# Moving operands of the two dense layers begin at twelve other columns, in tiles 128 columns wider

## The chip, the cores and the metric

The kernel runs on one core of a Trainium2 chip. The metric is the device time of one execution in microseconds; lower is better. The kernel before was run three times.

## The reference

Three stages follow each other. The first is a recurrent attention over 768 steps for 4 batches and 8 heads of 48; its result, 3072 tokens by 384, goes through two dense layers with 2048 hidden columns each.

```python
for t in range(S):
    cur = np.einsum('bhd,bhe->bhde', u[None] * kt, vt)
    y[:, :, t] = np.einsum('bhd,bhde->bhe', rt, state + cur)
    state = wt[:, :, :, None] * state + np.einsum('bhd,bhe->bhde', kt, vt)
...
h = x @ w_in;  g = np.maximum(h, 0.0) + alpha * np.minimum(h, 0.0);  x = g @ w_out
h = x @ w_in;  g = h * np.clip(h + 3.0, 0.0, 6.0) / 6.0;             out = g @ w_out
```

## The kernel before

**Tiling.** Tokens run in six blocks of 512 (`TB`), j = 0 to 5, through each of the two dense layers, m = 0 and 1. The 2048 hidden columns run in 16 slices of 128. Every float32 operand of a dense product is split into a high part, rounded to the format float32r, and the low rest, so that one product of 128 rows by 128 columns of weights with 512 tokens is three matmuls in `mm3` (lines 765 to 767): high by high, high by low, low by high. A slice of a block ("slot") needs three row groups of `x` for its hidden tile `h` (nine matmuls) and three column groups for its output `acc` (nine more). That makes 18 matmuls a slot, 288 a block, 1728 a layer.

**Operands.** The weights stay in 32 tiles of [128, 2, 384] 4-byte words, high and low part one behind the other, which the second layer's weights later replace. The moving operands are the activation tiles `xt` and `x2` of [128, 3, 2, 512] (two buffers, tag "xt"), and the gate tile `g` of [128, 2, 512] (three buffers). In each matmul the stationary operand is a 128-column piece of a weight tile, loaded by an LDWEIGHTS of its own while the matmul ahead of it streams its 512 columns.

**Where the tiles lie.** All pools lie one behind the other along each partition, and the widths between the first weight tile and the tiles that stream are multiples of 128 words (768 a weight tile, 384 a work tile, 512 a staging tile, 3072 an activation tile, 4 x 544 for the tiles ahead of `g`). So each moving operand of a dense layer and each 128-column piece of weights begin at the same column, counted modulo 128. Below, "distance" is the first column of the streaming operand less the first column of the weights that are loaded meanwhile, modulo 128: it is 0 for all 3456 dense matmuls. Other pairs have other distances. When a burst of attention follows a dense matmul, the next weights are a state tile `sbd` of 112 columns (line 588, `y<-kr,sbd`), and the four of these tiles stand at distances 120, 8, 24 and 40 from the streaming `xt`.

**Order.** The order of all instructions is made beforehand by a planner (`Plan`) from costs and due times; each engine then runs its own list. During layer 0 the attention of the next block (units of 256 tokens by two heads) is woven between the slots: `A<-kr` (line 477), `y<-kr,sbd` (588), `y<-X,v` (595, 599). A result `y` is split into the two parts of `xt` by ACT (635) and DVE (641), and a quarter of it goes there by DMA (651). In each slot ACT and DVE turn `h` into `g` (lines 801 or 803, 808 or 812, 818, 821) while PE works on other slots. From line 699 on, checks of the weights' range run during layer 0, from loads of their own.

Of the kernel before, what the change touches and what calls it, by code (L numbers as in the profile page):

```python
# [8 lines left out]
F32R = mybir.dt.float32r  # L9
# [11 lines left out]
P = 128  # L21
# [9 lines left out]
NK = DM // P  # L31
# [5 lines left out]
TB = 512  # L37
NB = NT // TB
AHEAD = 8
WARM = 400  # L40
FUSE = 16
U0, U1, W0 = -3.9, 2.0, -0.82


# [72 lines left out]
class Plan:  # L117
# [42 lines left out]
    def run(self):  # L160
        ops = self.ops
        for o in ops:
            o["left"] = len(o["full"]) + len(o["order"])
            for d in o["full"] | o["order"]:
                ops[d]["out"].append(o["id"])
        ready = {e: [] for e in ("PE", "DVE", "ACT", "POOL", "SP")}
        free = {e: self.BEGIN[e] for e in ready}

        def release(o):
            at = {e: 0.0 for e in o["where"]}  # L170
            for d in o["full"]:
                p = ops[d]
                for e in o["where"]:
                    wait = self.SAME[e] if e == p["eng"] else self.LATENCY
                    at[e] = max(at[e], p["end"] + wait)
            for d in o["order"]:
                for e in at:
                    at[e] = max(at[e], ops[d]["start"])
            o["t"] = at
            for e in o["where"]:  # L180
                ready[e].append(o)

        for o in ops:
            if not o["left"]:
                release(o)
        seq = []
        pair = 0.0

        def earliest(e, o):
            t = max(free[e], o["t"][e])  # L190
            return max(t, pair) if e == "POOL" or (e == "DVE" and o["pair"]) else t

        while True:
            best = None
            for e, lst in ready.items():
                if lst:
                    t = min(earliest(e, o) for o in lst)
                    if best is None or t < best[0]:
                        best = (t, e)
            if best is None:  # L200
                break
            t, e = best
            o = min(
                (o for o in ready[e] if earliest(e, o) <= t),
                key=lambda o: (o["due"] + (self.SPARE if o["flex"] and e == "DVE" else 0), o["id"]),
            )
            for x in o["where"]:
                ready[x].remove(o)
            d = o["where"][e] * (2 if e == "PE" and t < self.COLD else 1)
            o["eng"], o["start"], o["end"] = e, t, t + d  # L210
            free[e] = t + d
            if self.LOCK and (e == "POOL" or (e == "DVE" and o["pair"])):
                pair = t + d
            if e == "SP":
                o["end"] = t + d + 2.0
            if not (o.get("filler") and self.started):
                seq.append(o)
            else:
                o["end"] = t
                free[e] = t  # L220
            if o.get("starts"):
                self.started = True
            for x in o["out"]:
                ops[x]["left"] -= 1
                if not ops[x]["left"]:
                    release(ops[x])
        return seq


def fast_path(es, tc, unit, tok, vch, ub, w1, w2, alpha, out, flag, alp, x2d):  # L230
# [4 lines left out]
    xp = es.enter_context(tc.tile_pool(name="xp", bufs=2))  # L235
# [68 lines left out]
    XT, xt_buf, xt_ops = {}, {}, {}  # L304
# [49 lines left out]
    def add_unit(n):  # L354
        t, pr = divmod(n, NPAIR)
# [248 lines left out]
        def add_output(due=d + 2, more=0.0, then=None, after=(), use=()):  # L604

            def both(e):
                pc(e)
                if then:  # L610
                    then(e)

            o_pc = plan.op(
                {"PE": (0.8 if first else 1.02) + more}, due, both, need + list(after), new=[yb2],
                use=[krb, xb, vb] + sb + list(use),
            )

            j, off = t // 2, t % 2 * TH
            if j not in xt_buf:
                xt_buf[j] = plan.buf("xt", 2)  # L620
            ops = xt_ops.setdefault(t, [])
            cs = slice(off, off + TH)
            x3b = plan.buf("x3", 1) if pr == 3 else None

            def parts():
                if j not in XT:
                    XT[j] = xp.tile([P, NK, 2, TB], F32R, tag="xt", name=f"xt{j}")
                if pr < 3:
                    return XT[j][0:PR, pr, 0, cs], XT[j][0:PR, pr, 1, cs]
                if "x3" not in u:  # L630
                    u["x3"] = ap_.tile([PR, 2, TH], F32R, tag="x3", bufs=1, name=f"x3_{t}")
                return u["x3"][:, 0], u["x3"][:, 1]

            def hi_(e):
                nc.scalar.activation(
                    parts()[0], u["y"], AF.Copy, accum_out=sum_y[0:PR, n : n + 1]
                )

            def lo_(e):
                hi, lo = parts()  # L640
                nc.vector.tensor_tensor(out=lo, in0=u["y"], in1=hi.bitcast(F32), op=ALU.subtract)

            fresh = [xt_buf[j]] + ([x3b] if x3b else [])
            o_hi = plan.op({"ACT": 0.36}, d + 2.5, hi_, [o_pc], new=fresh, use=[yb2])
            o_lo = plan.op({"DVE": 0.35}, d + 2.5, lo_, [o_hi], new=fresh, use=[yb2])
            ops += [o_hi, o_lo]

            if pr == 3:

                def spread(e, h, i):  # L650
                    nc.sync.dma_start(
                        XT[j][48 + 64 * h : 64 + 64 * h, i, :, cs].bitcast(F32),
                        u["x3"][64 * h + 16 * i : 64 * h + 16 * i + 16].bitcast(F32),
                    )

                before = list(ops)
                for h in range(2):
                    for i in range(NK):
                        ops.append(
                            plan.op(  # L660
                                {"SP": 0.48}, d + 2.6, lambda e, h=h, i=i: spread(e, h, i),
                                before, use=[xt_buf[j], x3b],
                            )
                        )
            return o_pc

        if FUSE <= n + 1 < NU:
            waiting.append(add_output)
# [92 lines left out]
    acc_t, acc_buf, X2, x2_ops, x2_buf, x2d_ops = {}, {}, {}, {}, {}, {}  # L761
# [7 lines left out]
    def add_slot(m, j, f):  # L769
# [6 lines left out]
        k = {}  # L776
# [18 lines left out]
        def fresh(tag, bufs, shape, dtype=F32):  # L795
            return mp.tile(shape, dtype, tag=tag, bufs=bufs, name=f"{tag}{s}")
# [17 lines left out]
                )  # L814

        def ghi(e):
            k["g"] = fresh("g", 3, [P, 2, TB], F32R)
            nc.scalar.activation(k["g"][:, 0], k["p"], AF.Copy)  # L818

        def glo(e):  # L820
# [4 lines left out]
        o_q = plan.op({"ACT": 0.58}, s + 1.1, pq, [o_h, o_alpha], new=[qb], use=[hb])  # L825
        o_g = plan.op({"DVE": 0.62}, s + 0.8, gate, [o_q], new=[pb], use=[qb, hb])
        o_1 = plan.op({"ACT": 0.52}, s + 1.0, ghi, [o_g], new=[gb], use=[pb])
        o_2 = plan.op({"POOL": 1.23, "DVE": 0.61}, s + 1.2, glo, [o_1], use=[pb, gb], pair=True)

# [42 lines left out]
    def add_x2(j):  # L872
        due = NB * NF + NF * j - 6
        x2_buf[j] = plan.buf("xt", 2)
        x2_ops[j] = []
        for i in range(NK):
            sb = plan.buf("st", 4)
            k = {}

            def load(e, i=i, k=k):  # L880
                k["raw"] = xp.tile([P, TB], F32, tag="st", bufs=4, name=f"x2r{j}_{i}")
                nc.sync.dma_start(k["raw"], x2d[j, i])

            def hi(e, i=i, k=k):
                if j not in X2:
                    X2[j] = xp.tile([P, NK, 2, TB], F32R, tag="xt", name=f"x2_{j}")
                nc.scalar.activation(X2[j][:, i, 0], k["raw"], AF.Copy)

            def lo(e, i=i, k=k):
                xt = X2[j]  # L890
                eng[e].tensor_tensor(
                    out=xt[:, i, 1], in0=k["raw"], in1=xt[:, i, 0].bitcast(F32), op=ALU.subtract
                )

            o = plan.op({"SP": 0.75}, due + i, load, [x2d_ops[0, j, i]], new=[sb])
            o = plan.op({"ACT": 0.52}, due + 1 + i, hi, [o], new=[x2_buf[j]], use=[sb])
            o2 = plan.op(
                {"POOL": 1.25, "DVE": 0.61}, due + 2.2 + i, lo, [o], use=[x2_buf[j], sb]
            )
            x2_ops[j] += [o, o2]  # L900
# [291 lines left out]
```

## Time and profile before

| | us |
|---|---|
| median of 3 runs | 952.91 (952.12 to 954.6) |
| the profiled execution | 951.98 |
| its span in the profile | 950.1 |
| PE busy | 921.2 (97%) |
| DVE busy, ACT busy | 558.2, 531.8 |

What lies outside the span is 1.9 us. The 40 slices of the page show PE near full in all but the first; the granted clock of TensorE is full from the start of the dense layers to the last slice. ACT and DVE are about two thirds busy in the first half and one third in the second, in which only the second dense layer runs (about 543 to 945 us).

### The profile page before, as it was taken

The page shows a single profiled execution, that of the slowest core. Times are in us where ns is not written, and L with a number is a line of the kernel's source. Part 1 is how long each engine was busy: PE and PEld are TensorE (multiplying, and loading weights), DVE is VectorE, ACT ScalarE, POOL GpSimd, SP SyncE. Part 2 cuts the span into 40 slices and gives each one's busy share as a digit, 9 for nine tenths or more (in the row PEclk, how much of TensorE's full clock was granted, in tenths as well). Part 3 has the DMA queues.
Part 4 walks back from the last instruction along what each step waited for, and adds up shares of the span by engine and source line. Part 5 has one row for each costly group of instructions (what it writes and reads, how often), then busy time and mean ns, then how long its engine had stood idle before and what let it go on. Part 6 is the DMA issues. An engine that isn't in the chain of part 4 may idle for free.

```text
span 950.1 us, 13762 instructions
## 1 busy us (share of the span) xinstructions
PE 921.2 (97%) x4914; PEld 744.5 (78%) x4914; DVE 558.2 (59%) x1085; ACT 531.8 (56%) x1267; POOL 133.0 (14%) x133
## 2 busy tenths in 40 slices
PE   8799989999999999989999999999999999999996
PEld 5676767878887888777888888888888888888885
DVE  8999997565655656665359887343343433433332
ACT  6888776565656657877368886343333433433331
POOL 4323234121121201000012130000010000000000
PEclk9999999999999999999999999999999999999998
DMA  8788214122212215772046630010100100100001
GB/s 269 244 271 260 83 54 144 55 80 80 95 63 70 96 55 180 224 225 60 9 163 194 192 117 1 1 67 1 38 29 1 67 1 1 67 1 1 33 1 38
DMA packets 36750, 86.20 MB, mean 91 GB/s; under 512 B 5056, under 2 KB 7488, under 8 KB 36672
## 3 DMA queue, kind: packets, MB, share of 16 engines
q1 hardware_dynamic: 36672, 85.22, 28.6%
q8 instruction: 41, 0.67, 0.3%
q14 instruction: 37, 0.30, 0.1%
HBM read 73.41 MB, written 9.44 MB: 87 GB/s over the span
## 4 chain that ended last, share of the span: by engine, by line
PE 53%; DMA 4%; DVE 2%; ACT 1%; issue 1%; DVEq 0%; ACTq 0%
PE acc L765 9%; PE acc L766 9%; PE acc L767 9%; PE h L765 9%; PE h L766 9%; PE h L767 9%; DMA raw<-in_w 4%; DVE wv L112 1%; ACT junk L710 0%; DVE pg L808 0%; PE y L595 0%; DVE g L821 0%; PE A L477 0%; PE y L588 0%; DVE X L499 0%
## 5 line engine op out<-in xcount | busy, mean ns | idle before, releaser
L765 PE MATMUL acc<-g,w 128*128 128x512 f32 x576 | 228.9, 397 | 0.0
L767 PE MATMUL acc<-g,w 128*128 128x512 f32 x576 | 224.6, 390 | 0.0
L766 PE MATMUL acc<-g,w 128*128 128x512 f32 x576 | 224.5, 390 | 0.0
L821 DVE TENSOR_TENSOR g<-pg,g 128x512 fp32r<-128x512 f32 x175 | 122.7, 701 | 139.5 <-ACT g L818 139.4
L818 ACT ACTIVATE g<-pg 128x512 fp32r<-128x512 f32 x192 | 120.8, 629 | 146.4 <-PE acc L767 142.2
L803 ACT ACTIVATE q<-h,three 128x512 f32<-128x512 f32 x96 | 66.1, 688 | 123.8 <-PE h L767 123.8
L812 DVE SCALAR_TENSOR_TENSOR pg<-q,h 128x512 f32<-128x512 f32 x96 | 65.9, 687 | 112.3 <-ACT q L803 112.1
L765 PEld LDWEIGHTS acc<-g,w 128*128 128x128 f32 x576 | 108.1, 188 | 23.5 <-issue 0.4
L767 PEld LDWEIGHTS acc<-g,w 128*128 128x128 f32 x576 | 108.1, 188 | 22.8
L766 PEld LDWEIGHTS acc<-g,w 128*128 128x128 f32 x576 | 108.2, 188 | 21.5 <-DVE g L821 0.3
L765 PE MATMUL h<-xt,w 128*128 128x512 f32 x288 | 116.2, 404 | 1.5 <-ACT w L738 1.4
L767 PE MATMUL h<-xt,w 128*128 128x512 f32 x288 | 113.2, 393 | 0.2 <-DVE w L742 0.2
L766 PE MATMUL h<-xt,w 128*128 128x512 f32 x288 | 112.2, 390 | 0.0
L808 DVE SCALAR_TENSOR_TENSOR pg<-h,q 128x512 f32<-128x512 f32 x96 | 66.0, 688 | 78.4 <-ACT q L801 78.4
L765 PE MATMUL h<-x,w 128*128 128x512 f32 x288 | 112.0, 389 | 0.0
L766 PE MATMUL h<-x,w 128*128 128x512 f32 x288 | 112.0, 389 | 0.0
L767 PE MATMUL h<-x,w 128*128 128x512 f32 x288 | 112.0, 389 | 0.0
L801 ACT ACTIVATE q<-h,nal 128x512 f32<-128x512 f32 x96 | 65.4, 682 | 58.8 <-PE h L767 58.5
L423 POOL TENSOR_TENSOR kr<-un,tg 112x512 f32<-112x512 f32 (+1 forms) x43 | 43.4, 1012 | 233.0 <-PE y L588 201.5
L765 PEld LDWEIGHTS h<-xt,w 128*128 128x128 f32 x288 | 54.9, 191 | 13.0 <-ACT w L738 2.1
L767 PEld LDWEIGHTS h<-xt,w 128*128 128x128 f32 x288 | 54.0, 188 | 13.6 <-DVE w L742 1.7
L765 PEld LDWEIGHTS h<-x,w 128*128 128x128 f32 x288 | 54.1, 188 | 11.3
(93 smaller groups left out, 1268.1 us busy)
## 6 DMA issues: line engine op xcount, KB each, us to landing
wraw<-in_w SPq DMA_DIRECT2D x64, 384.0 KB, 3.9
un<-in_unit SPq DMA_DIRECT2D x48, 337.3 KB, 3.4
raw<-in_w SPq DMA_DIRECT2D x32, 384.0 KB, 3.7
rk<-in_tok SPq DMA_DIRECT2D x24, 384.0 KB, 3.9
v<-in_vch SPq DMA_DIRECT2D x12, 384.0 KB, 3.7
x2d<-st SPq DMA_DIRECT2D x18, 256.0 KB, 2.3
x2r<-x2d SPq DMA_DIRECT2D x18, 256.0 KB, 3.2
out<-st SPq DMA_DIRECT2D x18, 256.0 KB, 2.1
```

The lines of the kernel that those rows point to most:

```text
L112: nc.vector.tensor_scalar(v, weight_bits(raw)[0], 27, 15, op0=ALU.logical_shift_right, op1=ALU.bitwise_and)
L423: eng[e].tensor_tensor(out=u["kr"][:, i].rearrange("p a (c s) -> p a c s", c=2), in0=u["in"][:, 0 : 2 * TH].rearrange("p (a c s) -> p a c ...
L765: nc.tensor.matmul(ps, whi, xhi, start=start, stop=False, skip_group_check=True)
L766: nc.tensor.matmul(ps, whi, xlo, start=False, stop=False, skip_group_check=True)
L767: nc.tensor.matmul(ps, wlo, xhi, start=False, stop=stop, skip_group_check=True)
L801: nc.scalar.activation(q, k["h"], AF.Relu, scale=nal[:, f : f + 1])
L803: nc.scalar.activation(q, k["h"], AF.Relu, bias=three)
L808: nc.vector.scalar_tensor_tensor(out=p, in0=k["h"], scalar=0.0, in1=k["q"], op0=ALU.max, op1=ALU.subtract)
L812: nc.vector.scalar_tensor_tensor(out=p, in0=k["q"], scalar=6.0, in1=k["h"], op0=ALU.min, op1=ALU.mult)
L818: nc.scalar.activation(k["g"][:, 0], k["p"], AF.Copy)
L821: eng[e].tensor_tensor(out=k["g"][:, 1], in0=k["p"], in1=k["g"][:, 0].bitcast(F32), op=ALU.subtract)
```

## The change

Both kinds of moving tile become 128 words wider, and each block takes its operand from another start within the tile. `SHIFT` gives the start for layer m and block j. The weights stay where they are, and the wider tiles move the tiles behind them by multiples of 128 words, so the value in `SHIFT` is the new distance: 4, 8, 112, 0, 120, 124 for the blocks of layer 0, and 16, 32, 48, 64, 80, 96 for those of layer 1. The block j = 3 of layer 0 keeps distance 0. Both `xt` or `x2` and the `g` tiles of a block have the block's distance.

```diff
+SHIFT = ((4, 8, 112, 0, 120, 124), (16, 32, 48, 64, 80, 96))
...
+def shifted(tile_, m, j, n):
+
+    return tile_[:, SHIFT[m][j] : SHIFT[m][j] + n]
...
-                    XT[j] = xp.tile([P, NK, 2, TB], F32R, tag="xt", name=f"xt{j}")
+                    xt = xp.tile([P, NK * 2 * TB + P], F32R, tag="xt", name=f"xt{j}")
+                    XT[j] = shifted(xt, 0, j, NK * 2 * TB).rearrange(
+                        "p (k a t) -> p k a t", k=NK, a=2
+                    )
...
-            k["g"] = fresh("g", 3, [P, 2, TB], F32R)
+            g = fresh("g", 3, [P, 2 * TB + P], F32R)
+            k["g"] = shifted(g, m, j, 2 * TB).rearrange("p (a t) -> p a t", a=2)
...
-                    X2[j] = xp.tile([P, NK, 2, TB], F32R, tag="xt", name=f"x2_{j}")
+                    xt = xp.tile([P, NK * 2 * TB + P], F32R, tag="xt", name=f"x2_{j}")
+                    X2[j] = shifted(xt, 1, j, NK * 2 * TB).rearrange(
+                        "p (k a t) -> p k a t", k=NK, a=2
+                    )
```

On every engine the same instructions with the same shapes stand in the same order and wait for the same semaphores as before; only addresses differ.

## Rows read from the trace of the kernel before

**Rows 1.** The page: span, and busy time, share and instructions of PE.

```profile
span 950.1 us, 13762 instructions
PE 921.2 (97%) x4914; PEld 744.5 (78%) x4914; DVE 558.2 (59%) x1085; ACT 531.8 (56%) x1267; POOL 133.0 (14%) x133
```

**Rows 2.** Busy time by stretch, with instructions, granted clock, DMA share and GB/s.

```profile
core 0: us, PE busy (x) PEld busy (x) DVE busy (x) ACT busy (x) POOL busy (x), PEclk, DMA share, GB/s
...
160.00:227.00 67.00, 66.70 (x398) 53.42 (x397) 37.97 (x80) 39.16 (x108) 11.65 (x11) 1.00 0.22 67
...
393.00:460.00 67.00, 62.81 (x376) 50.59 (x374) 38.84 (x84) 48.21 (x138) 5.46 (x5) 1.00 0.45 136
...
607.00:673.00 66.00, 66.00 (x293) 54.66 (x292) 25.08 (x37) 23.50 (x37) 1.29 (x1) 1.00 0.07 24
```

**Rows 3.** The chain that ended last: its shares, and two of its pieces.

```profile
PE 53%; DMA 4%; DVE 2%; ACT 1%; issue 1%; DVEq 0%; ACTq 0%
...
404.61 5.05 DMA raw<-in_w
...
414.27 4.89 DMA raw<-in_w
```

**Rows 4.** The costliest groups: the dense matmuls, with count, busy time, mean ns.

```profile
L766 PE MATMUL acc<-g,w 128*128 128x512 f32 x576 | 224.5, 390 | 0.0
...
L766 PE MATMUL h<-x,w 128*128 128x512 f32 x288 | 112.0, 389 | 0.0
```

**Rows 5.** Timeline of PE from 696 us: start, duration, line, operation.

```profile
696.10 0.19 PE L928 MATMUL cnt<-ones,chk_s 128*1 128x1 f32 x2
696.22 0.50 PE L765 MATMUL acc<-g,w 128*128 128x512 f32 x1
696.55 0.39 PE L766 MATMUL acc<-g,w 128*128 128x512 f32 x1
696.78 0.40 PE L767 MATMUL acc<-g,w 128*128 128x512 f32 x1
697.01 0.40 PE L765 MATMUL acc<-g,w 128*128 128x512 f32 x1
697.25 0.39 PE L766 MATMUL acc<-g,w 128*128 128x512 f32 x1
697.47 0.39 PE L767 MATMUL acc<-g,w 128*128 128x512 f32 x1
...
698.63 0.39 PE L766 MATMUL h<-x,w 128*128 128x512 f32 x1
```

**Rows 6.** Timeline of PE near 700 us: the first and the last of 21 matmuls.

```profile
700.45 0.39 PE L765 MATMUL acc<-g,w 128*128 128x512 f32 x1
...
704.98 0.39 PE L767 MATMUL acc<-g,w 128*128 128x512 f32 x1
```

**Rows 7.** Timeline of PE: a run of 12 small matmuls in the prologue, at full clock.

```profile
46.35 1.48 PE L682 MATMUL warm<-ident 128*128 128x256 bf16 x12
```

**Rows 8.** The small matmul's own duration: ns min/median/max.

```profile
L682 PE MATMUL warm<-ident x128: 270/273/421, 1.4 to 51.6; 128*128 128x256 bf16 x128
```

**Rows 9.** Weight loads by shape: count, busy time, mean ns.

```profile
L766 PEld LDWEIGHTS acc<-g,w 128*128 128x128 f32 x576 | 108.2, 188 | 21.5 <-DVE g L821 0.3
...
L599 PEld LDWEIGHTS y<-X,v 128*48 128x48 f32 x192 | 18.6, 123 | 0.0
```

**Rows 10.** Timeline of PE at 220 us: a dense matmul, then the attention's first.

```profile
220.05 0.40 PE L767 MATMUL h<-xt,w 128*128 128x512 f32 x1
220.28 0.38 PE L588 MATMUL y<-kr,sbd 112*112 112x128 f32 x2
```

**Rows 11.** Line 767 just ahead of line 588, one at a time: ns min/median/max.

```profile
L767 PE MATMUL h<-xt,w x1: 397/397/397, 220.0 to 220.0; 128*128 128x512 f32 x1
...
L767 PE MATMUL h<-xt,w x1: 396/396/396, 178.0 to 178.0; 128*128 128x512 f32 x1
...
L767 PE MATMUL h<-xt,w x1: 389/389/389, 209.4 to 209.4; 128*128 128x512 f32 x1
...
L767 PE MATMUL h<-xt,w x1: 391/391/391, 230.5 to 230.5; 128*128 128x512 f32 x1
```

**Rows 12.** Who waited for whom: total us, times, longest.

```profile
ACT q L803 <- PE h L767: 123.8, 90, 1.5
```

**Rows 13.** DMA issues: count, KB each, median us to landing.

```profile
xt<-x SPq DMA_DIRECT2D x72, 32.0 KB, 2.1
```

## The prediction

> **What bounds the kernel now.** I read the page's head first: PE is busy for 921.2 of 950.1 us [rows 1]. The table by stretch then shows where that holds. In the second layer, stretch by stretch, PE is busy for the whole of it while DVE and ACT need 25.08 and 23.50 of 66 us [rows 2], and the waits put ACT behind PE, not the other way round (`q` waited 90 times for `h`) [rows 12]. In layer 0 PE is also nearly full (66.70 of 67 us), except around 393 to 460 us, where it is idle for 4.2 of 67 us [rows 2]; there the chain that ended last runs through loads of weights for the range check, two of them 5.05 and 4.89 us long, and not through matmuls [rows 3]. So nearly everywhere the time is a number of dense matmuls times their spacing, and the change has only that spacing to act on: no instruction, shape, order or wait differs.
>
> The duration shown for a matmul, 389 or 390 ns [rows 4], is not its spacing, since one starts long before the one ahead has ended. The spacing is read from starts in the timeline: 20 steps from 700.45 to 704.98 us are 4.53 us, 0.2265 us a step [rows 6]. As a check, a block of 288 at that spacing is 65.2 us, and the six blocks of layer 1 take 391 us, which is the stretch from 543 to 935 us. At the granted full clock, 2.4 GHz, 512 columns would stream in 0.2133 us. So each dense matmul carries about 13 ns over its columns, in each of 3456 matmuls 45 us in all. That is what the distance might touch.
>
> **What the trace says of these 13 ns.** Three rows bear on it.
>
> First, they are not the price of changing weights as such. Twelve small matmuls of 256 columns, each with its own load of 128 columns (bf16), take 1.48 us [rows 7]; less the 0.273 us of one [rows 8] that is 0.1097 us a step, 3 ns over 256 columns at full clock. The same 3 ns on 512 columns would be 0.2164 us.
>
> Second, the excess depends on how the weight load and the stream meet. After a small foreign matmul at 696.10 us the steps are 0.23, 0.23, 0.24, 0.22 us and so on, with durations of 0.39 and 0.40, and only after some ten steps do they settle at 0.2265 [rows 5, 6]. No operand changed its distance there. From 696.55 to 698.63 us nine steps take 2.08 us, 0.231 us each, 4.6 ns above the settled spacing. The settled state at distance 0 is thus among the cheap ones that this stretch shows; one step, from 697.25 to 697.47, is cheaper, by some 2 to 6 ns at the rounding of the rows.
>
> Third, other distances do stand in this trace, once per burst of attention: the dense matmul that streams `xt` while the 112 columns of `sbd` load [rows 10]. Its duration is 397 ns at distance 8 (220.0 us), 396 at 120 (178.0 us), 389 at 24 (209.4 us) and 391 at 40 (230.5 us) [rows 11], against 389 in the settled state at 0. Since a longer duration here goes with a later next start (0.40 against 0.39 in [rows 5]), I read the excess of the spacing from it: +8, +7, 0 and +2 ns. Three limits: the load is 112 columns and not 128, the weights are of another form, and it is the first step from a settled state, not a settled state itself.
>
> Why no distance should free the stream: a load of 128 columns takes 188 ns and one of 48 takes 123 [rows 9], so 80 columns more cost 65 ns, 0.81 ns a column; 128 columns are read in about 104 ns, and the stream passes some 250 of its columns meanwhile. The two reading points thus move apart by about 120 columns during one load, nearly the whole turn of 128 that the table covers. Whatever the start, they go through nearly all relative positions once. A collision between the two is moved to another time in the load by a shift, and its cost may change there; it is hardly avoided.
>
> The Trainium skill speaks against any of this: "TensorE: Matmul & The Clock Gate", Part 2, step 1, says that the stream and the weight load have independent read ports and that loading the next weights does not steal the matmul's bandwidth. By it the sum of this change is 0 and the time 952 us; the rows agree for the small bf16 matmuls and disagree for [rows 11], where the duration goes with the tile that is loaded.
>
> **The parts, each costed.** *Layer 1, distances 16 to 96.* 16 lies between 8 (+8) and 24 (0): I take +4. 32 lies between 24 and 40 (0, +2): +1. 48 is next to 40: +2. For 64, 80 and 96 the trace has nothing; between 0 and the 4.6 ns of the unsettled steps I take +2 each, since the rows nearest to them, 24 and 40, are low. The sum is 13 ns a matmul over six blocks, times 288, 3.7 us. PE is full here, so all of it shows. Bounds: 0, if each distance settles as 0 does, and 6 x 288 x 4.6 ns = 7.9 us.
>
> *Layer 0, distances 4, 8, 112, 0, 120, 124.* By nearness to 0 (0) and 8 (+8), 4 and 124 get +4; 8 gets +8; 112, which is 16 below 0, gets +4 as 16 does; block 3 gets nothing. Block 4 (120) would have +8, 2.3 us, but PE idles 4.2 us there behind the range check, which hides it; without that cover the 2.3 us show. The rest is 20 ns x 288 = 5.8 us. Bursts of attention unsettle the steps every few us in this layer, whatever the distance, so part of the excess is paid already: I take half, 2.9 us. Bounds: 0 and 8.1 us (all of it and block 4).
>
> *Everything else costs nothing.* ACT and DVE write the same shapes to shifted columns; they have some 40 us of slack in 66 [rows 2], and if their writes became a tenth longer the gates would still be early. The 72 transfers of 32 KB into `xt` [rows 13] start off the old boundaries; they land in 2.1 us and serve the next block, so even twice that stays hidden; if it did not, the first slot of a block would start 2 us late, 12 us in six blocks. The wider tiles move nothing else by part of a 128-word step.
>
> **The sum.** 3.7 + 2.9 = 6.6 us on the profiled execution's 951.98 us is 958.6. That execution lies 0.9 us below the median of the three runs, so I say 959. From the bounds, 0 to 16 us with the effect present, this case has its own range of 954.9 to 968.
>
> **The rivals.**
> *No effect (chance 0.22).* Every distance settles at the same spacing, because a shift in columns only alters where the ten unsettled steps begin. For it: the state at 696 us does come back to 0.2265 from any step, and the small sums above. Against it: nothing shows that the settled state at another distance is the same. Time 950 to 954.9 us, 952 by the profiled execution. The skill's rule on two ports gives the same time.
>
> *The stream is freed (0.34).* The 13 ns exist because weights and stream begin on the same column, and most other distances do without them, so that the spacing falls towards 0.2164 us. For it: the small matmuls pay 3 ns, not 13; the excess is the same to the nanosecond over all tiles, whose distance is always 0; the first step at 24 or 40 may hold a price for the change of form that hides a gain. Against it: the two points pass each other anyway, and no step at any of four distances was short. The price: 10.1 ns x 288 = 2.9 us a block; eleven blocks make 32 us, 920 us; only the six of layer 1 make 17.5 us, 934 us. Layer 0 would give back less near 393 us, where the loads decide. The skill states a spacing of 215.7 ns for back-to-back matmuls of 512 columns at full clock ("TensorE: Matmul & The Clock Gate", Part 1); by that figure eleven blocks would be an estimated 34 us faster, and no dense matmul here shows it.
>
> *Most distances stay at the worst step (0.08).* +8 to +9 ns in all eleven blocks: 3168 x 8.5 ns = 27 us, 979 us. It decides if the excess of 8 and 120 holds beyond 16 columns from 0, which 24 and 40 speak against.
>
> **The numbers.** The forecast has 0.36. A difference under 0.3%, 2.9 us, is about what a measurement of this kernel cannot tell from none. Faster is the freed stream, 0.34; same is no effect, 0.22; slower is the forecast and the worst step, 0.44. The range from 922 to 974 us leaves out the full freeing beyond 31 us and most of the worst case, some 0.15 together.
>
> **What would show it.** In the profile after, the spacing from starts, block by block: layer 1 at 0.227 to 0.231 us, the blocks of distance 8 and 4 in layer 0 above the one of distance 0, and block 3 of layer 0 unchanged. PE would be as full as now and the waits the same. I am wrong if a block at a distance other than 0 settles below 0.226, or if all settle at one spacing.

## The result and the profile after

The change makes the kernel slower: 962.72 us against 952.91 us in the median of three runs each, a ratio of 1.0097 (95% interval 1.0071 to 1.0124). The profiled execution after took 961.48 us, 9.5 us more than the one of before. The page's head:

```profile
span 959.7 us, 13762 instructions
PE 933.7 (97%) x4914; PEld 744.8 (78%) x4914; DVE 558.0 (58%) x1085; ACT 531.7 (55%) x1267; POOL 134.2 (14%) x133
```

PE does the same 4914 instructions in 12.5 us more [rows 1]; the busy times of DVE and ACT are unchanged to 0.2 us. Where the 9.6 us of span lie is seen from the first and last start of the hidden matmuls, `h<-xt` in layer 0 and `h<-x` in layer 1 (ns min/median/max, first and last start in us), after and then before:

```profile
L774 PE MATMUL h<-xt,w x288: 388/394/506, 52.5 to 543.3; 128*128 128x512 f32 x144
...
L774 PE MATMUL h<-x,w x288: 388/394/404, 546.0 to 942.2; 128*128 128x512 f32 x144
...
L765 PE MATMUL h<-xt,w x288: 387/389/504, 54.7 to 540.3; 128*128 128x512 f32 x144
...
L765 PE MATMUL h<-x,w x288: 389/389/393, 543.0 to 932.3; 128*128 128x512 f32 x144
```

So the prologue, up to the first of these starts, was 2.2 us shorter (in the kernels below, which all have the same prologue, it takes from 53.1 to 57.6 us), layer 0, from there to the first start of layer 1, took 5.2 us more (493.5 against 488.3) and layer 1 took 6.9 us more (396.2 against 389.3). The median duration of a hidden matmul went from 389 to 394 ns.

Layer 1 takes 389.3 us also in the two kernels below that have it at distance 0 or 64 throughout. Layer 0 varies more: in the profiles of the six kernels below that have it at distance 0 or 64 throughout it took from 486.9 to 492.7 us. So the 5.2 us alone would show little. PE's busy time in that stretch is the steadier number (before, then after):

```profile
54.68:543.00 488.32, 478.52 (x2739) 381.94 (x2740) 336.35 (x683) 331.68 (x860) 93.61 (x83) 1.00 0.41 126
...
52.48:546.02 493.54, 483.45 (x2739) 381.93 (x2740) 337.19 (x682) 331.69 (x860) 94.89 (x84) 1.00 0.41 125
```

It rises by 4.9 us for the same 2739 instructions, and in five of those six kernels it lies between 478.3 and 478.7 us. In the sixth, the last one below, it is 480.3 us, and the granted clock fell to 1.2 GHz once in layer 0.

The timeline of PE shows the spacing of each block of layer 1. For each block stand the first and the last of 37 matmuls in a row, 36 steps, in the order of distances 16, 32, 48, 64, 80, 96:

```profile
576.94 0.39 PE L776 MATMUL h<-x,w 128*128 128x512 f32 x1
...
585.18 0.39 PE L776 MATMUL h<-x,w 128*128 128x512 f32 x1
...
643.26 0.39 PE L776 MATMUL h<-x,w 128*128 128x512 f32 x1
...
651.63 0.40 PE L776 MATMUL h<-x,w 128*128 128x512 f32 x1
...
710.12 0.39 PE L774 MATMUL h<-x,w 128*128 128x512 f32 x1
...
718.52 0.39 PE L774 MATMUL h<-x,w 128*128 128x512 f32 x1
...
777.16 0.39 PE L776 MATMUL h<-x,w 128*128 128x512 f32 x1
...
785.32 0.39 PE L776 MATMUL h<-x,w 128*128 128x512 f32 x1
...
842.83 0.39 PE L776 MATMUL h<-x,w 128*128 128x512 f32 x1
...
851.07 0.39 PE L776 MATMUL h<-x,w 128*128 128x512 f32 x1
...
909.16 0.39 PE L776 MATMUL h<-x,w 128*128 128x512 f32 x1
...
917.52 0.40 PE L776 MATMUL h<-x,w 128*128 128x512 f32 x1
```

36 steps take 8.24, 8.37, 8.40, 8.16, 8.24 and 8.36 us. That is 228.9, 232.5, 233.3, 226.7, 228.9 and 232.2 ns a step. Starts are shown to 0.01 us, which leaves up to 0.3 ns in these numbers, so 32 and 96 may be equal; [rows 6], over 20 steps, gave 226.5 for distance 0, and 36 steps give 226.7 in other kernels at distance 0 below. The excess over 226.7, summed over the six blocks, is 22.3 ns, and times 288 it is 6.4 us of the 6.9 us.

### The profile page after: what moved, and what is told of

It is laid out like the page before. It is cut to its first block, busy times and chain, and to the rows that moved or that the text cites. A ratio compares the mean times of both kernels' runs of the same rounds, so it can differ in the third digit from the quotient of the medians.

```text
span 959.7 us, 13762 instructions
## 1 busy us (share of the span) xinstructions
PE 933.7 (97%) x4914; PEld 744.8 (78%) x4914; DVE 558.0 (58%) x1085; ACT 531.7 (55%) x1267; POOL 134.2 (14%) x133
## 4 chain that ended last, share of the span: by engine, by line
PE 53%; DMA 4%; DVE 2%; ACT 1%; issue 1%; DVEq 0%; ACTq 0%
PE acc L774 9%; PE acc L776 9%; PE acc L775 9%; PE h L774 9%; PE h L776 9%; PE h L775 9%; DMA raw<-in_w 4%; DVE wv L113 1%; ACT junk L719 0%; DVE pg L817 0%; ACT q L810 0%; ACT g L828 0%; PE y L601 0%; PE A L483 0%; PE y L594 0%
## 5 line engine op out<-in xcount | busy, mean ns | idle before, releaser
L776 PE MATMUL acc<-g,w 128*128 128x512 f32 x576 | 226.5, 393 | 0.0
L831 DVE TENSOR_TENSOR g<-pg,g 128x512 fp32r<-128x512 f32 x175 | 122.3, 699 | 144.0 <-ACT g L828 143.8
L774 PE MATMUL h<-x,w 128*128 128x512 f32 x288 | 113.4, 394 | 0.0
L776 PE MATMUL h<-x,w 128*128 128x512 f32 x288 | 113.2, 393 | 0.0
L775 PE MATMUL h<-x,w 128*128 128x512 f32 x288 | 112.9, 392 | 0.0
L776 PEld LDWEIGHTS h<-x,w 128*128 128x128 f32 x288 | 54.1, 188 | 12.5
```

The costliest lines, as they stand in the source:

```text
L774: nc.tensor.matmul(ps, whi, xhi, start=start, stop=False, skip_group_check=True)
L775: nc.tensor.matmul(ps, whi, xlo, start=False, stop=False, skip_group_check=True)
L776: nc.tensor.matmul(ps, wlo, xhi, start=False, stop=stop, skip_group_check=True)
L831: eng[e].tensor_tensor(out=k["g"][:, 1], in0=k["p"], in1=k["g"][:, 0].bitcast(F32), op=ALU.subtract)
```

## The experiments

Theory 1 is that the distance between the streaming operand and the weights sets the spacing of dense matmuls. Its rivals are the operand's own start, and the place of a block in the program. A second question is to what the 13 ns over the streaming time belong. Where a time has no interval, it is from a single run.

**The table's rows exchanged.**

```diff
-SHIFT = ((4, 8, 112, 0, 120, 124), (16, 32, 48, 64, 80, 96))
+SHIFT = ((16, 32, 48, 64, 80, 96), (4, 8, 112, 0, 120, 124))
```

> The two rows of the table are exchanged: layer 1 gets 4, 8, 112, 0, 120, 124 and layer 0 gets 16 to 96. Theory 1 (the distance between the streaming operand and the weights that are loaded sets the spacing): in layer 1 the spacing goes with the number and not with the block, 226.7 ns at 0 and 124, 231 to 234 ns at 4, 8, 112 and 120, about 7 us over six blocks; the whole near 962 us. Theory 2 (the place of a block in the program sets it): layer 1 keeps the spacings that its blocks had, 229, 232, 233, 227, 229, 232 ns in this order.

Measured: 965.62 us, 1.0129 of before (1.0097 to 1.0161). Blocks with distance 4, 0 and 124 in layer 1, 36 steps each:

```profile
580.06 0.40 PE L776 MATMUL h<-x,w 128*128 128x512 f32 x1
...
588.40 0.40 PE L776 MATMUL h<-x,w 128*128 128x512 f32 x1
...
780.98 0.39 PE L776 MATMUL h<-x,w 128*128 128x512 f32 x1
...
789.14 0.39 PE L776 MATMUL h<-x,w 128*128 128x512 f32 x1
...
913.62 0.39 PE L776 MATMUL h<-x,w 128*128 128x512 f32 x1
...
921.78 0.39 PE L776 MATMUL h<-x,w 128*128 128x512 f32 x1
```

They take 8.34, 8.16 and 8.16 us: 231.7 ns at 4, 226.7 at 0 and at 124. Read in the same way, 8, 112 and 120 stand at 233.3. The spacing goes with the number, not with the block; theory 2 falls. The whole is 3.6 us above the expected 962.

**Everything moved by 48 columns, distances kept.**

```diff
     junk = const.tile([P, DM], BF16, name="junk")
+    pad = const.tile([P, 48], F32, name="pad")
```

> The kernel before with 48 unused columns ahead of all tiles of weights, activations and gates: every start moves by 48 columns, every distance stays 0. Theory 1 (distance): 226.7 ns and the time of before, within 0.3%. Rival (the streaming operand's own start counts, whatever the weights): its start is now the one that it had at distance 48, so 233 ns in all 3456 matmuls, some 20 us slower, 973 us.

Measured: 953.44 us, ratio 1.0003 (0.9975 to 1.0030). In layer 1, 36 steps take 8.16 us, 226.7 ns:

```profile
618.14 0.39 PE L766 MATMUL acc<-g,w 128*128 128x512 f32 x1
...
626.30 0.39 PE L766 MATMUL acc<-g,w 128*128 128x512 f32 x1
```

The operand's own start costs nothing, and the rival falls.

**The weights alone moved by 48 columns.**

```diff
+    pad = const.tile([P, 48], F32, name="pad")
+    gap = wr.tile([P, 80], F32, tag="gap", bufs=1, name="gap")
```

The first line stands ahead of the weight tiles, the second behind them: 48 + 80 = 128.

> The kernel before with the weight tiles alone moved by 48 columns, the activations and gates start where they did: distance -48, which is 80 of 128. Theory 1: the spacing of distance 80 (and 16), 229 ns, everywhere: 2.4 ns by 3456 matmuls is 8 us at most, 956 to 961 us. Rival (the streaming operand's own start): 226.7 ns and 953 us.

Measured: 960.83 us, ratio 1.0084 (1.0055 to 1.0114). 36 steps take 8.24 us, 228.9 ns, the level of distance 80 above:

```profile
618.49 0.39 PE L768 MATMUL h<-x,w 128*128 128x512 f32 x1
...
626.73 0.39 PE L768 MATMUL h<-x,w 128*128 128x512 f32 x1
```

No activation or gate changed its start modulo 128 here, and still each block of layer 1 is slower. The difference of the two starts is what counts. "TensorE: Matmul & The Clock Gate" of the Trainium skill, Part 2, step 1, has loading the next weights take nothing from the running matmul. For these matmuls the measurement says otherwise: with only the loaded tiles moved, a step takes 228.9 instead of 226.7 ns.

**Twelve further distances.**

```diff
+SHIFT = ((12, 20, 28, 36, 40, 44), (1, 2, 3, 60, 62, 56))
```

> Twelve further distances: 12, 20, 28, 36, 40, 44 in layer 0 and 1, 2, 3, 60, 62, 56 in layer 1. If the spacing repeats every 64 columns, as 16 and 80, 32 and 96, 0 and 64 suggest, then 60 settles at 226.7 ns like 124, and 56 is at 233 ns like 120. If whole groups of 4 columns (16 bytes) count, 1, 2 and 3 read like 0 or 4; if single columns count they differ from both. Theory that some distance frees the stream: one of the twelve falls below 226 ns; theory that none does: all twelve lie between 226.6 and 234 ns.

Measured: 972.91 us, the slowest time of all. Distances 1, 3 and 60:

```profile
583.89 0.40 PE L776 MATMUL h<-x,w 128*128 128x512 f32 x1
...
592.46 0.40 PE L776 MATMUL h<-x,w 128*128 128x512 f32 x1
...
718.46 0.39 PE L774 MATMUL h<-x,w 128*128 128x512 f32 x1
...
726.70 0.39 PE L774 MATMUL h<-x,w 128*128 128x512 f32 x1
...
785.57 0.40 PE L776 MATMUL h<-x,w 128*128 128x512 f32 x1
...
794.09 0.40 PE L776 MATMUL h<-x,w 128*128 128x512 f32 x1
```

1 column off stands at 238.1 ns (8.57 us), 3 at 228.9 and 60 at 236.7 (8.52 us). Read in the same way, 2 and 56 stand at 233.3 and 62 at 231.1. So single columns count. The expectation that 60 reads like 124 was wrong (236.7 against 226.7 ns), and so was the upper bound of 234 ns; 56 came out as expected. None of the six of layer 1 is below 226.6. In layer 0, where bursts of attention seldom leave 36 dense steps in a row, only a mean can be given for a block: over the steps under 0.3 us from one dense matmul to the next it is 230.8 ns or more in each of the six.

**Distance 48 everywhere.**

```diff
+SHIFT = ((48,) * 6, (48,) * 6)
```

> Distance 48 for all twelve blocks. If the time is the number of dense matmuls times the spacing of their distance, 3456 steps at 233.3 instead of about 227.3 ns give 20 us more, 973 us, less up to 4 us that PE has idle near 400 us. If layer 0 hid its excess behind the loads and the attention, only layer 1 would show: 11 us more, 964 us.

Measured: 971.63 us, ratio 1.0207 (1.0170 to 1.0245). 36 steps take 8.40 us, 233.3 ns:

```profile
618.68 0.39 PE L776 MATMUL h<-x,w 128*128 128x512 f32 x1
...
627.08 0.39 PE L776 MATMUL h<-x,w 128*128 128x512 f32 x1
```

The span is 970.3 us, 20.2 above before. Layer 1 has 6 x 288 x 6.7 ns = 11.6 us of it. The rest, near 9 us, is layer 0 (497.1 against 488.3 us), so its excess does reach the end, and the second expectation, 964 us, falls. How much of another 11.6 us is hidden isn't shown: in this execution the granted clock was 0.50, that is 1.2 GHz, from 144.1 to 147.4 and from 434.2 to 437.5 us, after PE had been busy for 5.45 and 5.52 of the 7.00 us up to 143 and 434. In each 9 matmuls start where some 14 would have, an estimated 2.4 us in all, and the layer varies by some us between kernels.

**Layer 0 at 0, and six distances more in layer 1.**

```diff
+SHIFT = ((0,) * 6, (24, 40, 68, 12, 72, 127))
```

> Layer 0 at distance 0, layer 1 at 24, 40, 68, 12, 72, 127. Reading 1 (the first step of the attention's burst gives the settled spacing of the same distance): 24 at about 227 and 40 at about 229 ns. Reading 2 (it doesn't, the settled steps have a level of their own): 24 near 231 ns as its neighbours 20 and 28, 40 near 234 ns as in layer 0. If the table repeats every 64 columns, 68 reads like 4 (231.6 ns) and 72 like 8 (233.3 ns). No distance below 226.6 ns.

Measured: 963.71 us. Distances 24, 40 and 68:

```profile
575.53 0.40 PE L776 MATMUL h<-x,w 128*128 128x512 f32 x1
...
583.93 0.40 PE L776 MATMUL h<-x,w 128*128 128x512 f32 x1
...
642.87 0.39 PE L776 MATMUL h<-x,w 128*128 128x512 f32 x1
...
651.31 0.39 PE L776 MATMUL h<-x,w 128*128 128x512 f32 x1
...
709.91 0.40 PE L774 MATMUL h<-x,w 128*128 128x512 f32 x1
...
718.25 0.40 PE L774 MATMUL h<-x,w 128*128 128x512 f32 x1
```

24 stands at 233.3 ns and 40 at 234.4, where the first step behind a settled state [rows 11] had shown +0 and +2 ns. Reading 1 falls: the settled level is its own quantity. Reading 2 had 40 right and 24 some 2 ns too low. 68 is at 231.7 like 4, and 72 at 233.3 like 8; 12 is at 233.3 and 127 at 231.1.

**Half of the columns loaded.**

```diff
+            half = slice(i * P, i * P + P // 2) if m and f and j in (2, 3) else cs
+            to = acc_t[m, j, i][0 : P // 2] if m and f and j in (2, 3) else acc_t[m, j, i]
             mm3(
-                acc_t[m, j, i], wt[:, 0, cs], wt[:, 1, cs], g[:, 0], g[:, 1],
+                to, wt[:, 0, half], wt[:, 1, half], g[:, 0], g[:, 1],
```

> The kernel before; in blocks 2 and 3 of layer 1 the matmuls into acc, from the second slice on, take only 64 of the 128 columns of weights, so half of the output's rows there get the first slice alone. The streams stay 512 columns, the loads are half as long. If the 13 ns over 512 columns are paid to the reading of the loaded columns, steps under a half load fall towards 220 ns. If they are a fixed price of a change of weights at 512 float32r columns, they stay at 226.7 ns.

Measured: 954.87 us. The half loads are shorter (mean ns of one, by shape):

```profile
L767 PEld LDWEIGHTS h<-x,w 128*128 128x128 f32 x30 | 5.6, 188 | 1.3
...
L766 PEld LDWEIGHTS acc<-g,w 128*64 128x64 f32 x29 | 3.9, 135 | 2.7
```

but the steps are not. In the timeline the first row is a matmul during which a half load runs, the second is the first, nine steps on, that has a full load again, and the third, another nine steps on, has a half load:

```profile
701.77 0.39 PE L767 MATMUL h<-x,w 128*128 128x512 f32 x1
...
703.84 0.39 PE L767 MATMUL acc<-g,w 128*64 128x512 f32 x1
...
705.90 0.39 PE L767 MATMUL h<-x,w 128*128 128x512 f32 x1
```

Nine steps with half loads take 2.07 us, 230 ns each; at 220 they would take 1.98. The nine with full loads that follow take 2.06 us, 229 ns. So the excess does not go with the number of columns that are loaded. But the second expectation isn't met either: both kinds lie 2 to 3 ns above 226.7. That each change between full and half loads unsettles the steps, as the foreign matmul in [rows 5] does, fits this, but no run separates it.

**Each stream split in two.**

```diff
+            for c in (slice(0, TB // 2), slice(TB // 2, TB)):
+                nc.tensor.matmul(
+                    ps[:, c], w, x[:, c], start=start and n == 0 and c.start == 0,
+                    stop=stop and n == 2, skip_group_check=True,
+                )
```

> The kernel before; in blocks 2 and 3 of layer 1 each dense matmul is split into two of 256 columns, each with its own load of 128. If the excess belongs to the load, each half carries some 13 ns: 120 ns a step, 69 us a block instead of 65.3. If it belongs to the streamed columns, each half carries half of it: 113.3 ns a step, 65.3 us a block. If it comes with 512 columns alone, 110 ns a step and 63 us a block.

Measured: 962.73 us. Two slot halves of 18 steps follow each other:

```profile
704.99 2.32 PE L767 MATMUL acc<-g,w 128*128 128x256 f32 x18
707.15 2.32 PE L767 MATMUL h<-x,w 128*128 128x256 f32 x18
```

18 steps take 2.16 us, 120.0 ns a step. 256 columns at 2.4 GHz take 106.7, so 13.3 ns come on top, as with 512 columns: at both lengths the price is paid once per matmul. Each matmul here has a load of its own, and no run has float32r matmuls without one, so whether the price is that of the load or of the matmul itself is not shown. Small matmuls of the same 256 columns in bf16, with a load each, paid 3 ns [rows 7, 8]. That points to float32r, but they also read other tiles.

**Distance 64 everywhere.**

```diff
+SHIFT = ((64,) * 6, (64,) * 6)
```

> Distance 64 for all twelve blocks: with the table as measured so far (64 settles at 226.7 ns, as 0 does) the time is that of before within 0.3%, 953 us, though every moving tile is wider and starts elsewhere. If the wider tiles or another start cost something apart from the distance's own level, it is slower.

Measured: 952.95 us, ratio 0.9994 (0.9980 to 1.0007). 36 steps take 8.16 us, 226.7 ns:

```profile
618.32 0.39 PE L776 MATMUL h<-x,w 128*128 128x512 f32 x1
...
626.48 0.39 PE L776 MATMUL h<-x,w 128*128 128x512 f32 x1
```

Wider tiles and another start cost nothing by themselves.

**The gates of layer 1 alone at 48.**

```diff
+SHIFT = ((0,) * 6, (48,) * 6)
...
-                    X2[j] = shifted(xt, 1, j, NK * 2 * TB).rearrange(
+                    X2[j] = shifted(xt, 0, j, NK * 2 * TB).rearrange(
```

> Layer 0 and the activations of layer 1 at distance 0, the gates of layer 1 at 48: nine steps of a slot stream x, nine stream g. If each step pays for its own distance, the steps that stream x are at 226.7 and those that stream g at 233.3 ns, 950.1 plus 5.7 us in the span, 956 us. If a level has to settle over some ten steps of one distance, the nine steps on x don't reach 226.7 and stay near 231 ns: up to 9 us more, 959 us.

Measured: 962.1 us. The first start of nine steps on `x`, the sixth, the first of nine on `g`, and of the next on `x`:

```profile
720.60 0.39 PE L774 MATMUL h<-x,w 128*128 128x512 f32 x1
...
721.76 0.39 PE L776 MATMUL h<-x,w 128*128 128x512 f32 x1
...
722.66 0.39 PE L774 MATMUL acc<-g,w 128*128 128x512 f32 x1
...
724.76 0.39 PE L774 MATMUL h<-x,w 128*128 128x512 f32 x1
```

Nine steps on `x` take 2.06 us, 228.9 ns, and nine on `g` 2.10 us, 233.3 ns. Both expectations hold in part. Each step pays for its own distance, but behind the change of distance the first five steps on `x` take 1.16 us, 232 ns each, and only the last four, 0.90 us, 225 ns at the rounding of the rows, are back at the settled level. So settling took five steps here, not some ten, and costs 2.2 ns a step over the nine. From the first to the last start, layer 1 takes 7.4 us more than before (396.7 against 389.3). That the whole exceeds both expectations lies in layer 0: it took 492.7 against 488.3 us at the same distance 0, with a granted clock of 0.50 (1.2 GHz) from 144.0 to 147.3 us, after PE had been busy for 5.36 of the 7.00 us up to 143.

## Why the prediction was right, point by point

**What bounds the kernel.** Right. Kernels that share every instruction range from 953 to 973 us by addresses alone, and in each the spacing of dense matmuls moved with the time; apart from it, the prologue and the waits in layer 0 vary by some us between executions.

**That distance 0 is a cheap state, and no other frees the stream.** Right, and now shown over 24 distances in layer 1 (those of the table, of its exchange and of the two further sets): none settles below 226.6 ns, 0, 64 and 124 reach 226.7, the others lie between 228.9 and 238.1. The rival of the freed stream is out for these 24 of 128 distances, and that of no effect too.

**The worst step at most distances, given 0.08.** It was nearer than that. Its condition, that the excess of 8 and 120 holds beyond 16 columns from 0, is met: of the 24 distances 12 stand at 233.3 ns or above, 24, 40, 48, 56 and 72 among them. That the sum of this change stayed well under the 27 us of that rival is in part luck, since its table has five of the six distances (0, 64, 124, 16 and 80, not 3) at which a step costs 2.2 ns or less. The sign for layer 1, 0.227 to 0.231 us, held for 16, 64 and 80 and failed for 32, 48 and 96, at 0.232 to 0.233. The signs for layer 0 held: the mean of the steps under 0.3 us from one dense matmul to the next is 231.9 ns at 4, 233.1 at 8 and 228.6 in block 3, which had 228.4 before.

**The reason given for it.** The picture of two reading points that pass each other in every load did not hold up in the form that I used: with half the columns loaded the excess should have shrunk, and it did not. Nor does its first reading carry over: it took from the bf16 matmuls that the 13 ns are not the price of changing weights as such, but each float32r matmul, of 256 columns or of 512, carries them. What the runs show is a price per matmul with its load, 13.3 ns at the best distances, and up to 11 ns more by the distance. Why a distance of 1 costs 11 ns, 3 costs 2 and 64 nothing stays open; no run here separates the two accesses further.

**Layer 1, 3.7 us.** It was 6.9. This is the mis-sized term, and its step was the reading of [rows 11]: the duration of the one dense matmul ahead of the attention's first, taken for the settled spacing. It served at 8 and 120 (+8 and +7 read, +6.6 settled) and failed at 24 and 40 (+0 and +2 read, +6.6 and +7.7 settled), so 32, 48 and 96, at +1, +2 and +2, were too low (+5.8, +6.6, +5.5 measured) and 16 and 64 too high (+4 and +2, against 2.2 and 0).

**Layer 0, 2.9 us.** It was 5.2, of which 4.9 us are PE's busy time. With the settled levels of its distances (231.7 at 4, 233.3 at 8, 112 and 120, 226.7 at 0 and 124) the full excess would be 7.1 us, so that halving for the unsettled steps was too much. The cover of block 4 did not show either. The stretch from 393 to 460 us after:

```profile
393.00:460.00 67.00, 62.25 (x366) 49.20 (x366) 38.56 (x86) 48.55 (x140) 5.87 (x5) 1.00 0.47 142
```

PE is busy for 62.25 us in it against 62.81 in [rows 2], with 10 instructions fewer. Its idle time did not shrink, as it would have if slower steps had filled it: it became 4.75 instead of 4.19 us. From 388 to 446 us PE waits for `X` and `Y` of the attention, which DVE writes, for 4.9 us before and 4.7 after, and DVE waits most of all for the loads, 10.7 and 9.8 us. Why slower steps did not fill these waits is not shown.

**Everything else at nothing.** Right: with distance 64 the time is that of before to 0.06% (0.9980 to 1.0007), and with the table of this change the busy times of DVE and ACT stay as they were.

**The sum.** 3.7 + 2.9 was 6.6 us. The profiled execution gave 6.9 + 5.2 = 12.1 us, less 2.2 us of a shorter prologue and 0.3 at the end, 9.6 us of span. So both terms were too small, by almost half together, and a prologue that the change does not touch brought the whole nearer to the forecast by chance. The 12.1 us lie inside the range that the forecast's own bounds had, 0 to 16 us.

## What to carry to other kernels

Where float32r matmuls with a load of weights each fill PE, the spacing of their starts, not the duration shown, is the number to read, and it can hang on how far apart the two operands begin: in these kernels 0 and 64 columns modulo 128 were the safe choices, and the spacing is worth measuring after any change that alters a tile's width. A single step out of a settled state is a poor sample of the settled level; settling took ten steps in [rows 5] and five behind a change of distance. One kernel that gives each block another start measures six or twelve such cases in one run.

## What was not expected of the hardware

The price of a float32r matmul with its load is the same 13.3 ns at 256 and at 512 streamed columns, and it is no lower with half loads (230 ns a step, against 229 with full loads in the same slots). The levels are nearly periodic in 64 columns (0 and 64 at 226.7; 16 and 80 at 228.9; 4 and 68 at 231.7; 8 and 72 at 233.3 ns), but 60 and 124 differ by 10 ns. And a shift of one column, 4 bytes, is the worst that was seen: 238.1 ns a step, 5% above distance 0.
